# Attention and mixer in one kernel: the first unit gets a home of its own, and the five engine queues are drawn anew

## The chip, the cores and the metric

The kernel runs on one core of a Trainium2 chip. The metric is the device time of one execution in microseconds (us), as the median of several runs. TensorE is called PE here, VectorE DVE, ScalarE ACT, GpSimd POOL and SyncE SP, as in the profile. All arithmetic is fp32; the mixer's weights arrive as 64-bit floats and are turned into fp32 on the chip.

## The reference

There are two stages. The first is a delta-rule attention with 4 batches, 8 heads, 768 steps and head size 48: a state of 48 x 48 for each head, updated step by step. The second takes its output as tokens x of 4 x 768 x 384.

```python
k_n = k / (np.linalg.norm(k, axis=-1, keepdims=True) + 1e-06)
for t in range(S):
    y[:, :, t] = np.einsum('bhd,bhde->bhe', q[:, :, t], state)
    v_old = np.einsum('bhde,bhd->bhe', state, kt)
    state = state + bt[..., None] * np.einsum('bhd,bhe->bhde', kt, vt - v_old)
# x: y with the heads side by side, (4, 768, 384)
h = x.transpose(0, 2, 1) @ U @ V              # U (768, 32), V (32, 768)
u = x + h.transpose(0, 2, 1)
out = u + np.maximum(u @ w_ch1, 0.0) @ w_ch2  # 384 -> 1536 -> 384
```

## The kernel before

**Attention.** The work is cut into eight units: unit n is half of the sequence (`hf`) of batch `b`, n = 2b + hf, with six chunks of 64 steps for each of its heads. A unit loads k, q, v and z (k in the layout of the state update), takes norms (`norms`: a sqrt on ACT, L611, and the rest on DVE from L614), and forms two grams, k with k and q with k (`grams`): six matmuls by the identity turn a pair of chunks (L668), ACT copies the result into the unit's slot (L682), 24 calls of small matmuls form the products (L704), and DVE masks them (L717, L736). `blocks` inverts the unit lower triangular blocks: 30 pairs of DVE operations (L790, L796), transposes (L781, L803, L812), and joins on PE (L847 to L908) with ACT copies (L895, L914, L926). Then a recurrence over the chunks of each batch runs on PE (L972, L986, L1066, L1090, L1107, L1135) with DVE (L1120, L1147, L1149) and ACT (L956) between the steps. It writes the tokens into `X`.

**Weights.** The mixer's weights come in 14 slices (L1221: slice 0 is U and 1 is V, 2 to 7 are `w_ch1`, 8 to 13 `w_ch2`) into rotating rooms, by POOL's queue for slice 0 and by SP's for the others. DVE (L1244, L1250, L1256, L1262, L1272) and ACT (L1229) convert them; L1272 writes them into `w1_sb` and `w2_sb`. The loads of a slice are entries of part 78 up to `78.13`, its conversion an entry 14 higher (`78.21` is slice 7).

**Mixer.** There are twelve tiles of 256 tokens, three for each batch. A tile has a front (L1469 for the first tile of a batch, L1476 and L1486, the addition L1495 on DVE, and turning on PE at L1514 or, in quadrants, L405, with the ACT copy L1517 into `ut`), a wide product (L1580, or L393 in quadrants), a narrow product (L1695 or L393), and a sum L1620 with the store. The last five tiles take the first product in fewer steps (L1430), with sums of weights made on DVE. The matmuls run in several layouts of the PE array: full 128 rows, quadrants of 64, quarters of 32.

**Order.** Every engine works its instructions off in the order in which they stand in its queue. The program is written as about a hundred generators, the parts, each numbered. `ORDER` is a table with five queues, one for each engine, whose entries are numbers of parts: each entry lets that part issue its next operation on that engine. `11.2*2` is two operations of the third part that part 11 has started. A part waits in `need(...)` until keys such as `("rec", 0)` (batch 0's recurrence is done) or `("x", 0, c)` (a chunk's tokens are written) have been emitted. The order is thus fixed when the program is built; on the chip semaphores make the data dependences. The set `PARTED` lists the parts that use quadrants where both forms exist.

**Slots.** Two tiles of 9792 words for each partition hold a unit's data: `slots[n % 2]`. A unit's loads, in `load`, therefore wait for the unit two before:

```python
yield need(("rec", n - 2), ("used", n - 2), *[("x", b - 1, UC * hf + c) for c in range(UC)])
```

Units 0 and 2 share a slot, so unit 2's loads are issued at 80.5 to 90.3 us. The mixer's transposed tokens live in a rotating pair of tiles named `ut`.

Of the kernel before, what the change touches and what calls it, by code (L numbers as in the profile page):

```python
# [8 lines left out]
FP32 = mybir.dt.float32  # L9
# [9 lines left out]
DP = 64  # L19
# [7 lines left out]
def kernel(  # L27
# [68 lines left out]
    def dve(n):  # L96
        return (n + 151) / 960.0
# [16 lines left out]
    def need(*keys):  # L114
        return [key for key in keys if key[1] >= 0]
# [12 lines left out]
    def advance(i, value, at):  # L128
# [20 lines left out]
        9.0 9.1 9.0.0.0 9.1.0.0 2*2 19.0 19.1 3 19.0.0.0 3 19.1.0.0 10.0 10.1 10.0.0.0 20.0 11.4 10.1.0.0  # L149
        11.4 11.2*2 11.4*2 11.2*2 20.1 11.4*4 20.0.0.0 11.2*4 20.1.0.0 4.1 4.0*2 4.1 21.2*2 4 4.4 21.2 4  # L150
        21.2 4.5 4 21.4*2 21.2 4 4.5 4.6 4*2 21.2 4.6 21.2*2 4.7 4*2 4.8 4.7 4 21.4 4.9 4 21.4 4 4.9 4.8
        4.2*2 21.4*2 4 4.10 21.4*2 4*2 4.10 4.11 4*2 4.11 4.3 32.0 31.0 4.3 31.1 4.12 4 31.0.0.0 31.1.0.0 4
        4.12 32.1 4.13 4*2 4.13 4.14 4 4.15 4 4.14 4.15 79 32.0.0.0 81 32.1.0.0 81*2 40.0 82 98.0*2 39.0
        39.1 82 98.1 40.1 39.1.0.0 39.0.0.0 98.1 98.2 33.2*2 98.2 98.3*2 98.4 33.4*2 33.2 98.4 33.2 98.5
        33.4*2 33.2*2 98.5 98.7 83 33.2 33.4 33.2 33.4 98.7 33.4*2 98.8 5 5.0 5 40.1.0.0 5 98.8 5.1 5 98.9 5
        98.9 5 5.1 98.9 5 98.9 5.2 5 98.10 5 5.2 5.3 5 99.0 5 99.0 5 5.3 5.4 5 99.0 5 99.0 5.5 5 99.1*2 5
        5.4 99.1*2 5.5 40.0.0.0 5 83 99.2*2 99.3*2 99.4 48.0 99.4 41.2*2 47.0 99.7 47.1 47.0.0.0 47.1.0.0
        41.4*2 99.5*2 48.1 41.2 41.4*2 41.2 99.7 99.8 48.1.0.0 5 99.8 5.6 5 48.0.0.0 5 99.9 5 99.9 5.7 5*2
        99.9 5 5.6 99.9 5.8 5.7 5 99.10 5*2 100.0 5.9 5 100.0 5.8 5 100.0 5 100.0 5.9 5 5.10 5 100.1 5.11 5
        5.10 100.1 5 5.11 100.1*2 84 100.2*2 100.3*2 100.4*2 100.5 100.7 100.5 49.2*2 55.0.0.0 84 55.1.0.0  # L160
        100.7 100.8 49.2 49.4*2 49.2 100.8 84 100.9*2 6 85 100.9 6 100.9 56.0.0.0 56.1.0.0 6 100.10 49.4*2
        6.0 6 101.0*2 85 6.1 6 101.1*2 6 101.1 6 101.1 6.2 6 101.2*2 6.1 6 101.2*2 6 6.3 6.2 101.3 6 101.3 6
        6.4 6.3 6 101.4 6 101.4 6.5 6 101.4 6 101.4 6.4 6 6.5 101.5*2 101.7*2 57.2*2 57.4*2 86 57.4*2 57.2*2
        101.8*2 101.9*2 63.0.0.0 101.10 6 101.10 6 63.1.0.0 102.0*2 86 6.6 6 102.1*2 64.0.0.0 6 6.6 102.2 6
        102.2 6.7 6 102.2*2 6 6.7 102.3 6 102.3 6.8 6 102.3 6 102.3 6.9 6 102.4 6 102.4 6.8 6 102.4 6 102.4
        6.10 6 102.5*2 6.9 6.11 102.5 6 102.5 6.10 6 102.7 6.11 102.7 87 102.7*2 64.1.0.0 87 102.8*2 102.9*2
        102.10 71.0.0.0 103.0*2 71.1.0.0 103.1*2 103.2*2 103.3*2 65.4*2 65.2*2 103.4*2 72.1.0.0 65.2*2
        65.4*2 103.5*2 87 103.7 7 72.0.0.0 7 103.7 7 7.0 103.8*2 7.1 7 103.8*2 7 88 7 103.9*2 7 7.1 7.2 7
        103.10 7 7.2 104.0 7 104.0 7.3 7 104.0*2 7 7.3 7.4 104.1 7 104.1 7 104.1*2 7.5 7 7.4 104.2 7 104.2
        88 104.3*2 7 7.5 73.4*2 73.2*2 104.4*2 104.5 73.4*2 73.2*2 104.5 7 104.7 7 7.6 7 104.7 7 7.7 104.8  # L170
        7.6 7 104.8 7 104.8 7 104.8 7 7.7 7.8 7 104.9 7 7.8 7.9 7 104.9 7 89 7 104.10 7 7.9 7.10 7 7.11 7
        104.10 7 7.10 7.11 79 93.2 93.1 79 89 93.4 93.2 93.1 93.3 93.2 93.3 93.4 93.1 93.5 93.1 93.2 93.1
# [12 lines left out]
        78.20*2 21.4 78.21 21.4 78.21*4 4 78.22*2 4 78.22*2 4 78.22 4 78.23*2 4 78.23*3 78.24*5 4 78.25*2
        31.0.0.0*2 31.1.0.0*2 4 33 4 30 4 78.25 4 33*2 4 78.25*2 33*2 78.26 32.0.0.0 78.26 81 33 78.26 81
        32.1.0.0*2 78.26 33 78.26 33 82 33*2 32.0.0.0 30 33*8 33.4 33.2 78.26.1*3 39.0.0.0 78.27 98.2.1*3
        39.1.0.0 78.26.1 39.0.0.0 30 78.27*4 39.1.0.0 33.2*3 33.4*2 78.27.1 33.4 41 98.5.1*2 78.27.1*2
        98.7.0 98.5.1 78.27.1 38 83 41 98.6 5 98.7.1 41*3 38 98.8.0 5 98.8.1 41*3 5 41 5 41*2 40.1.0.0
        98.9.0 41 98.9.1 5 40.1.0.0 41 98.10.0 5 41*2 5 41 5 41*2 5 41 5 41*15 41.2 5 99.2.1 40.0.0.0 99.2.1  # L190
        38 40.0.0.0 99.2.1 99.7.0 41.4 47.0.0.0*2 47.1.0.0*2 49 99.5.1*3 46 49*2 46 49*2 99.7.1 99.8.0 99.6
        5 48.1.0.0*2 99.8.1 49*2 48.0.0.0 5 48.0.0.0 49 5 49*2 5 49*2 5 99.9.0 49*2 99.9.1 49 99.10.0 5 49 5
        49*2 5 49 5 49*2 5 49 5 49*9 46 49*2 84 49 100.2.1*2 49.2 49.4 55.1.0 55.0.0 100.5.1*2 100.2.1
        100.5.1 100.7.0 84 55.1.0.0 55.0.0.0 55.1.0.0 100.7.1 55.0.0.0 100.6 57 100.8.0 54 100.8.1 56.0.0
        57*4 56.1.0 6 85 100.9.0 56.0.0.0 56.1.0.0 56.0.0.0 6 57 56.1.0.0 100.9.1 100.10.0 57*7 6 57 6 57*2
        6 57*2 6 57*3 101.2.1 57 6 57 6 57*2 6 57 6 57*5 6 54 57*3 57.2 101.2.1 101.7.0 57.4 101.2.1
        101.5.1*3 101.7.1 54 86 101.6 101.8.0 101.8.1 63.0.0 64.0.0 101.9.0 101.9.1 63.1.0 63.0.0.0 6
        63.0.0.0 101.10.1 101.10.0 64.1.0 63.1.0.0*2 65 62 65*2 6 65 64.0.0.0 62 6 64.0.0.0 65*2 6 65*2 6
        65*3 6 65 6 102.2.1 65 6 65 6 65*3 6 102.2.1*2 65 6 65 102.5.1*2 65 62 87 65 102.5.1 102.7.0 65*3
        102.7.1 65 102.8.0 65 102.6 102.8.1 87 65 102.9.0 65 71.0.0 65 102.9.1 102.10.0 64.1.0.0*2 71.1.0  # L200
        65*4 71.1.0.0 65 71.0.0.0 65.4 71.0.0.0 71.1.0.0 65.2 73 72.1.0 72.0.0 70 73*2 72.1.0.0 103.2.1 73
        72.1.0.0 73*3 103.2.1*2 73 103.7.0 103.5.1*2 72.0.0.0 73 7 103.5.1 103.7.1 73 72.0.0.0 7 73 103.6
        73*2 7 103.8.0 88 103.8.1 73 7 73*2 103.9.0 73*2 7 73 103.10.0 103.9.1 7 73*2 7 73*2 7 73*2 70 7
        73*3 7 73*6 73.2 73.4 7 70 80*3 104.2.1*2 80 104.2.1 104.5.1 7 80*2 93.0*2 104.5.1 7 104.7.0 104.5.1
        104.7.1 7 104.6 7*2 93.0 104.8.0 104.8.1 7 93.0 104.9.0 7 80 7 104.9.1 7 89 93.0 7*2 93.0*2 80
        93.0*2 80*2 93.0 80 104.10.0 80 93.2.1 94.0*3 80 93.1.1 93.0 80 93.3.1 93.2.2 93.1.2 93.1.3 104.10.1
        93.2.3 93.5.0 94.0 93.1.4 94.0*6 93.4.1 90 94.2.1 90 105.0*3 94.3.1 94.1.1 105.1 94.1.2 94.2.2
        105.1*2 105.3.1 105.3.0 95.0 94.1.3 95.0*4 94.5.0 94.2.3 95.0 105.4.0 94.0 105.2 94.4.1 95.0 105.4.1
# [1568 lines left out]
```

## Time and profile before

| | |
|---|---|
| time, median of 3 runs | 590.49 us (590.03 to 590.49) |
| profiled execution | 589.15 us, span 587.4 us |
| mean granted PE clock | 0.939 |
| busy: PE, DVE, ACT, POOL | 545.3, 456.2, 227.3, 118.1 us |
| first DVE operation of batch 0's recurrence (L1149) | 59.47 us |
| its last (L1120) | 110.89 us |
| first front, L1469 | 113.50 us |
| first wide product, L1580 | 121.49 us |

Times within the profile are counted from the first instruction of the span. A line such as `L790` is the line of the kernel that issued the instruction. In a list of waits, the engine that stood idle is to the left of the arrow and what released it to the right, followed by the sum, the number and the longest.

### The profile page before, as it was taken

What the parts mean: (1) busy time and instruction counts of PE and PEld (TensorE: products, weight loads), DVE (VectorE), ACT (ScalarE), POOL (GpSimd) and SP (SyncE); (2) the same over time, 40 slices, a digit from 0 to 9 for tenths busy, and PEclk for the clock granted to TensorE, in tenths of its full rate; (3) what the DMA queues carried; (4) which work ended last, traced back from release to release, by engine and by line L of the source; (5) the groups of instructions that cost most, each with busy time, mean ns of one, the idle gap of its engine ahead of it and who ended that gap; (6) DMA issues with size and microseconds to landing.
All of it is one profiled execution on the core that took longest, in us unless ns stands there. A gap on an engine that the chain in (4) does not pass through costs nothing.

```text
span 587.4 us, 25542 instructions
## 1 busy us (share of the span) xinstructions
PE 545.3 (93%) x11460; PEld 491.1 (84%) x11460; DVE 456.2 (78%) x1086; ACT 227.3 (39%) x483; POOL 118.1 (20%) x205
## 2 busy tenths in 40 slices
PE   5697778799999999999999999999999999999997
PEld 4586677588888987997897798988889999999997
DVE  6898999999899898899878888888547574555552
ACT  4447476544433623344344305324423422131220
POOL 8132050311205304340252253301000000000000
PEclk9576666799999999999999999999999999999999
DMA  9634676652104314223212433200000000000013
GB/s 157 85 76 128 192 188 166 134 91 63 29 4 83 68 22 83 74 53 63 48 30 61 80 75 71 60 29 3 2 5 1 2 1 1 1 2 1 1 42 119
DMA packets 79213, 35.17 MB, mean 60 GB/s; under 512 B 65600, under 2 KB 76992, under 8 KB 79104
## 3 DMA queue, kind: packets, MB, share of 16 engines
q1 hardware_dynamic: 71200, 24.10, 18.9%
q0 software_dynamic: 6304, 9.15, 7.2%
q8 instruction: 90, 1.47, 1.0%
q10 hardware_dynamic: 1600, 0.30, 0.3%
q14 instruction: 19, 0.16, 0.1%
HBM read 28.80 MB, written 4.72 MB: 57 GB/s over the span
## 4 chain that ended last, share of the span: by engine, by line
PE 79%; DVE 7%; ACT 5%; DMA 4%; issue 3%; SPq 1%; POOL 1%; DVEq 0%; ACTq 0%; POOLq 0%
PE P L1695 24%; PE P L1580 12%; PE P L1430 12%; PE P L393 10%; PE P L704 3%; DMA wide<-in_moe_w_ch_dram 2%; PE P L668 2%; PE P L1066 2%; PE P L1090 1%; PE P L972 1%; PE P L1486 1%; PE P L986 1%; PE P L1135 1%; PE P L1514 1%; PE P L861 1%
## 5 line engine op out<-in xcount | busy, mean ns | idle before, releaser
L1695 PE MATMUL P<-w_sb,hs 128*128 128x192 f32 x480 | 84.2, 329 | 0.1
L1580 PE MATMUL P<-ut,w_sb 128*128 128x256 f32 x348 | 81.8, 386 | 0.1
L1695 PEld LDWEIGHTS P<-w_sb,hs 128*128 128x128 f32 x480 | 77.7, 190 | 1.3 <-issue 0.3
L1580 PEld LDWEIGHTS P<-ut,w_sb 128*128 128x128 f32 x348 | 64.1, 190 | 9.4 <-issue 0.6
L796 DVE TENSOR_TENSOR xt<-xt,prod 128x112 f32<-128x112 f32 (+21 forms) x200 | 64.6, 323 | 6.9
L790 DVE TENSOR_TENSOR prod<-gs,xt 128x112 f32<-128x112 f32 (+21 forms) x200 | 63.7, 319 | 3.9
L1620 DVE TENSOR_TENSOR X<-X,P 128x192 f32<-128x192 f32 x86 | 29.6, 349 | 36.1 <-PE P L1695 34.2
L1545 ACT ACTIVATE hs<-P 128x512 f32<-128x512 f32 x42 | 24.8, 597 | 62.1 <-PE P L1580 51.0
L393 PE MATMUL P<-ut,w_sb 64*64 64x256 f32 x624 | 43.0, 384 | 1.2 <-ACT hs L1545 0.9
L956 ACT COPY X<-P 64x192 f32<-64x192 f32 x96 | 30.0, 312 | 28.8 <-PE P L986 27.2
L704 PE MATMUL P<-slot 48*64 48x64 f32 x1536 | 33.5, 245 | 1.9 <-ACT slot L682 1.6
L704 PEld LDWEIGHTS P<-slot 48*64 48x64 f32 x1536 | 30.0, 157 | 6.1 <-ACT slot L682 2.5
L933 POOL MEMSET slot<- 32x384 f32 x32 | 13.4, 420 | 102.6 <-PE P L890 40.4
L1412 DVE TENSOR_TENSOR hs<-hs,P 128x512 f32<-128x512 f32 x30 | 20.1, 684 | 17.5 <-PE P L1430 9.2
L1695 PE MATMUL P<-w_sb,S 128*128 128x192 f32 x192 | 33.7, 330 | 0.0
L926 ACT COPY slot<-zz 32x384 f32<-32x384 f32 x64 | 32.3, 508 | 1.0
L1099 ACT COPY z<-P 128x192 f32<-128x192 f32 x36 | 11.5, 319 | 53.3 <-PE P L1090 46.4
L1695 PEld LDWEIGHTS P<-w_sb,S 128*128 128x128 f32 x192 | 31.1, 190 | 0.6 <-DVE xt L796 0.3
L548 POOL DMA_DIRECT2D slot<-in_k_dram x44 | 28.7, 657 | 12.3 <-PE P L1135 10.6
L668 PE MATMUL P<-ident,slot 128*128 128x128 f32 x108 | 20.0, 343 | 11.3 <-DMA slot<-in_k_dram 5.7
L1430 PE MATMUL P<-slot 128*128 128x128 f32 x240 | 29.7, 276 | 0.0
L1695 PE MATMUL P<-w_sb,slot 128*128 128x192 f32 x168 | 29.1, 327 | 0.0
(171 smaller groups left out, 1140.9 us busy)
## 6 DMA issues: line engine op xcount, KB each, us to landing
out_dram<-X SPq DMA_DIRECT2D x22, 192.0 KB, 2.0
X<-in_moe_w_ch_dram SPq DMA_DIRECT2D x10, 384.0 KB, 4.4
wide<-in_moe_w_ch_dram SPq DMA_DIRECT2D x10, 384.0 KB, 4.4
slot<-in_k_dram SPq DMA_DIRECT2D x48, 72.0 KB, 3.7
slot<-in_k_dram POOLq DMA_DIRECT2D x44, 72.0 KB, 3.1
slot<-in_v_dram SPq DMA_DIRECT2D x32, 72.0 KB, 3.7
slot<-in_v_dram POOLq DMA_DIRECT2D x32, 72.0 KB, 3.2
hs<-in_moe_w_ch_dram SPq DMA_DIRECT2D x4, 384.0 KB, 5.7
```

What stands on the lines that cost most here:

```text
L393: nc.tensor.matmul(to[half(g)], w[half(r), half(g)], x[half(r)], start=start, stop=stop, skip_group_check=True,)
L548: queue.dma_start(out=t[half(1 - g if name == "z" else g), :, to, 0:D], in_=src[b, 4 * g + s, hf * UC * L : (hf + 1) * UC * L, :].rearrang ...
L668: nc.tensor.transpose(p_t[:, c // 3, c % 3], t[:, c, 2 * j : 2 * j + 2].rearrange("p s d -> p (s d)"), ident,)
L704: nc.tensor.matmul(p_g[half(g ^ (par * i)), par, c], kq[rows, c, j, 0, half(g)], kq[rows, c, j, i, half(g)], start=True, stop=True,)
L790: nc.vector.tensor_tensor(out=prod, in0=gb[:, :, j : j + 1, j + 1 :].to_broadcast([128, split, m, w]), in1=xb[:, :, 0:m, j : j + 1].to_bro ...
L796: nc.vector.tensor_tensor(out=xb[:, :, 0:m, j + 1 :], in0=xb[:, :, 0:m, j + 1 :], in1=prod, op=ALU.subtract,)
L926: nc.scalar.copy(pg[quarter(i), :, at, :, a : a + BK], cut(zc, h)[quarter(i)].rearrange("p r (c j) t -> p r c j t", j=2),)
L956: nc.scalar.copy(x[half(c % 2), c // 2, 4 * D * g : 4 * D * (g + 1)].rearrange("p (j r d) -> p r j d", r=2, d=D), states(p_y)[half(g)],)
L1430: nc.tensor.matmul(bank[:, q], w_block(w)[:, q // 2, 128 * (q % 2) : 128 * (q % 2) + 128], token(b, i, t), start=c == 0 and q == 0, stop=True,
L1580: nc.tensor.matmul(p_f[:, x], w(x, t), ut[:, t], start=(t == 0), stop=(t == KT - 1))
L1620: nc.vector.tensor_tensor(out=to, in0=to, in1=p, op=ALU.add)
L1695: nc.tensor.matmul(to, of[0], of[1], start=of[2], stop=of[3], skip_group_check=True)
```

## The change

The first unit no longer lives in slot 0. Its large arrays go into `w2_sb`, its q and v into a new constant tile `uts_sb`, and its z into the last slice of `w1_sb`. The rotating `ut` of the mixer becomes the two halves of `uts_sb`. Unit 2 has slot 0 to itself: its loads wait only for two memsets, which a new part `pads` issues on POOL (they clear the padding columns, which unit 0's memsets cleared before). The last step of the weight slices from number 7 on, which writes where unit 0 lives, waits for unit 0's end. All five queues and `PARTED` are drawn anew; part numbers from 80 on are one higher.

```diff
+    w1_sb = const.tile([128, FT // 2, KT * 256], FP32, name="w1_sb")
+    w2_sb = const.tile([128, PRODUCTS, HF, HD], FP32, name="w2_sb")
+    uts_sb = const.tile([128, 2, KT, GT], FP32, name="uts_sb")
+
-    def views(slot):
+    def views(slot, q_room=None, z_room=None):
+        q_room = slot[:, 7680:9216] if q_room is None else q_room
+        z_room = slot[:, 9216 : 9216 + 2 * UC * D] if z_room is None else z_room
...
     units = [views(slots[n % 2]) for n in range(N)]
+    units[0] = views(
+        w2_sb.rearrange("p a f d -> p (a f d)"), uts_sb.rearrange("p y t n -> p (y t n)"),
+        w1_sb[:, FT // 2 - 1, 0 : 2 * UC * D],
+    )
...
+    def pads():
+        yield op("pool", 0.6)
+        nc.gpsimd.memset(units[2][0][:, :, :, D:DP], 0.0)
+        yield op("pool", 0.6)
+        nc.gpsimd.memset(units[2][4][:, :, :, D:DP], 0.0)
+        emitted("pads", 0.1)
...
-        yield need(("rec", n - 2), ("used", n - 2), *[("x", b - 1, UC * hf + c) for c in range(UC)])
+        if n != NU:
+            yield need(("rec", n - 2), ("used", n - 2), *[("x", b - 1, UC * hf + c) for c in range(UC)])
+        else:
+            yield ["pads"]
...
             emitted(("freed", i))
+            if i >= 7:
+                yield need(("rec", 0), ("used", 0), *[("x", 0, c) for c in range(UC)])
             yield op("dve", dve(n), port=True)
...
-        ut = uts[b, i] = mix.tile([128, KT, GT], FP32, name="ut")
+        ut = uts[b, i] = uts_sb[:, (NG * b + i) % 2]
...
+        begin(pads(), 5)
```

In the queues, part 1 is unit 0's k with the warm-up sqrt, 2 is beta, 8 unit 0's norms, 9 and 10 its grams, 11 its blocks, 18 to 21 the same for unit 1, 30 to 33 for unit 2. Parts 12 to 17 load unit 0's q, v and z, 22 to 29 unit 1's k, q, v and z, and 34 to 37 unit 2's. The first lines of three queues, before and after:

```diff
         act="""
-        1*4 9.0.0 1 9.1.0 9.0.0.0 9.1.0.0 78.14.0 2*2 9.0.0.0*2 8 19.0.0 9.0.0.0 9.1.0.0*3 19.0.0.0 19.1.0
...
+        1*4 9.0.0 9.1.0 9.0.0.0 9.1.0.0*2 2*2 9.1.0.0 8 9.0.0.0*3 9.1.0.0 1 19.0.0 3 19.1.0 19.0.0.0 10.1.0
+        10.0.0 20.0.0 3 19.0.0.0 78.14.0 19.1.0.0*2 11.4.0 11.2 18 11.4 11.4.0 11.2.0*2 11.3*3 11.4 11.1
+        19.1.0.0 20.1.0 11.2 31.0.0 19.0.0.0 32.0.0 11.3 78.15.0 11.4 11.1*3 11.2*2 11.4 19.1.0.0 31.1.0
+        19.0.0.0 4.0 32.1.0 4.0 21.2.0 4.1*2 21.2 78.16.0 4.4*2 21.2.0 78.17.0 21.1 21.4 78.18.0 21.2 21.1
...
         pool="""
-        11.0 13 23 78.0 2*3 17 23 25 23 13 23 25 13*2 25 29 25 21.0 15*2 29 17 15*2 11.3 11.1 11.3 11.1 27*4
...
+        11.0 80 78.0 23 25 23 80 2*3 23 13 23 13 17 13 25 13 15 21.0 15 25 34 35*2 34 35 17 35 15 25 31.0 29
...
         sp="""
-        0*4 78.1 22*2 12*2 22*2 78.1*2 12 78.1 12 24*3 14*4 24 16 26*4 78.2*2 28 16 78.3*2 78.4*2 28 78.5*2
...
+        0*4 22 24 34 12 22*3 24 12*2 35 12 78.1 35 78.1 24 35 14 24 14 34 78.1 16 34 78.1 35 34 26 14*2 16
```

More of the change, by code (lines that the diff above doesn't have):

```diff
@@ new lines @@
+        33.4*2 33.2 99.5 99.7 33.2 99.7 33.4 33.2*2 84 33.4 5 5.0 5 33.4*2 99.8 5 99.8 5.1 5 40.1.0.0 5 99.9
+        5 99.9 5.1 5 99.9*2 5.2 5*2 99.10 5 5.2 5.3 5 100.0*2 5 5.3 100.0 5 100.0 5.4 5 100.1 5.5 5 5.4
+        100.1 5 100.1 5.5 100.1 5 40.0.0.0 100.2*2 100.3*2 84 100.4 48.0 100.4 41.2*2 47.0 47.1 100.7
+        47.1.0.0 47.0.0.0 41.4*2 100.5*2 48.1 41.2 41.4 41.2 41.4 100.7 100.8 48.1.0.0 5 100.8 48.0.0.0 5
+        5.6 100.9 5 100.9 5 100.9 5 5.7 5 100.9 5 5.6 100.10 5.7 5 5.8 5 101.0 5 5.8 5.9 101.0 5*2 101.0*2 5
@@ new lines @@
+        78.20 21.4 78.21 21.4 78.21 21.4 78.21*3 4 78.22*2 4 78.22*2 4 78.22 4 78.23*5 4 78.24*5 4 78.25
+        31.0.0.0 4 31.0.0.0 78.25 31.1.0.0*2 4 33 4 78.25 4 78.25 4 78.25 30 33*4 82 33*2 82 33*4 32.0.0.0
+        32.1.0.0 78.26 32.1.0.0 32.0.0.0 78.26*2 33*2 78.26 83 33 78.26 78.26.1 33*4 30 39.1.0.0*2 78.26.1
+        33.2 78.27*3 99.2.1 78.27 99.2.1 78.27 33.4 39.0.0.0 33.2*2 39.0.0.0 33.2 78.27.1 78.26.1 41 30
+        78.27.1 78.26.1 33.4 99.7.0 33.4*2 99.5.1 78.27.1 99.5.1 78.27.1 84 99.5.1 99.2.1 5 99.7.1 38 41*2
@@ new lines @@
+        101.6 101.8.0 101.8.1 54 57 56.0.0 57 86 56.1.0 6 101.9.0 57*2 6 56.0.0.0 56.1.0.0*2 101.9.1
+        101.10.0 57*8 56.0.0.0 6 57 6 57*2 6 57 6 57*2 6 57*3 6 57*4 6 57 6 57*7 57.4 57.2 102.7.0 102.2.1
+        102.5.1 102.2.1*2 6 102.5.1*2 54 102.7.1 87 54 102.6 102.8.0 102.8.1 63.0.0 102.9.0 63.1.0 64.0.0
+        102.9.1 63.0.0.0 6 63.0.0.0 63.1.0.0*2 102.10.1 65 102.10.0 62 64.1.0 65 6 65*2 6 64.0.0.0*2 6 65 6
+        65*5 6 65 6 65*2 6 65 6 65*2 103.2.1 6 65*2 6 65 103.2.1 65 103.2.1 103.5.1*2 65 103.5.1 65 103.7.0
@@ new lines @@
+        4.6 21.4.0 4.5 21.1 4.6 4.5 21.4.0 78.19.0 21.2*2 4.7*2 21.1 78.20.0 4.8*2 78.21.0 4.9*2 4.2*2
+        21.3*4 21.4 78.22.0 21.4*2 4.10*2 78.23.0 4.11 4.3*2 78.24.0 4.11 31.0.0.0 31.1.0.0 4.12*2 78.25.0
+        31.0.0.0 31.1.0.0 4.13 30 4.13 4.14 4.15*2 4.14 82 99.0.0 78.26.0 39.0.0 99.1.0 39.1.0 40.1.0 40.0.0
+        39.1.0.0 99.2.0 39.1.0.0 39.0.0.0 33.2 78.27.0 83 99.3.0 39.0.0.0 99.4.0 33.1 33.4 33.1*2 99.5.0
+        33.2 33.1 33.2*2 38 33.3 5 33.4*2 5.0 33.4 33.3*2 5.0 5 99.9 33.3 5 5.1*2 5 5.2 100.0 5.2 5.3*2 5
@@ new lines @@
+        26 78.2*2 26*2 78.3 36 78.3 36 78.4*2 78.5*2 78.6 36 78.6 78.7 28 78.7 78.8*2 78.9 28 78.9 78.10*2
+        78.11*2 78.12 37*2 78.12 78.13 43*2 36 42 78.13 42*3 43*2 44*4 45*2 50 51*4 99.10.0 50*3 52 53 52*3
+        111*8 59*2 99.9.1 58 53 59*2 61 59*3 61 58*3 59 60 100.9.1 60*2 101.9.1 60 112*8 67*8 102.9.1 66*2
+        69 68*3 100.10.0 101.10.0 113*8 66 75 77 68 75 77 75 102.10.1 74*2 69 75 66 75 74 75 74 75*2
+        103.10.0 76*4 104.10.0 103.9.1 104.9.1 110.3.1 106.6.0 107.5.1 105.10.1 108.6.0 109.5.1 106.5.1
@@ L439, in views @@
         qk = slot[:, 6144:7680].rearrange("p (r c j t) -> p r c j t", r=2, c=UC, j=2)
-        qn = slot[:, 7680:9216].rearrange("p (c s d) -> p c s d", c=UC, s=4)
-        vn = slot[:, 7680 : 7680 + CS * D].rearrange("p (c s d) -> p c s d", c=UC, s=4)
-        kz = slot[:, 9216 : 9216 + 2 * UC * D].rearrange("p (c j d) -> p c j d", c=UC, j=2)
+        qn = q_room.rearrange("p (c s d) -> p c s d", c=UC, s=4)
+        vn = q_room[:, 0 : CS * D].rearrange("p (c s d) -> p c s d", c=UC, s=4)
+        kz = z_room.rearrange("p (c j d) -> p c j d", c=UC, j=2)
         diag = slot[:, 6144 : 6144 + BK * BK].rearrange("p (q t) -> p q t", t=BK)
@@ L474 @@
     nc.vector.memset(beta_rows, 0.0)
-    w1_sb = const.tile([128, FT // 2, KT * 256], FP32, name="w1_sb")
     u_sb = const.tile([128, NB, R], FP32, name="u_sb")
     v_sb = const.tile([128, S], FP32, name="v_sb")
-    w2_sb = const.tile([128, PRODUCTS, HF, HD], FP32, name="w2_sb")
     hs = const.tile([128, FT, GT], FP32, name="hs")
```

177 lines of the change are left out of this document (73 added, 104 removed), and 3 rows, old and new, of the table pe.

## The prediction

> **What bounds the kernel now.** I read the page's slices first, then busy time by stretch, then the waits of DVE, the chain of waits, and the timelines of the places that the diff moves. The slices, 14.7 us each:
>
> ```profile
> PE   5697778799999999999999999999999999999997
> DVE  6898999999899898899878888888547574555552
> PEclk9576666799999999999999999999999999999999
> DMA  9634676652104314223212433200000000000013
> ```
>
> PE is full from the ninth slice (about 118 us) to the end. Ahead of that DVE is, with PE at a low clock. The stretches say it in us (columns: length, busy time of PE, PEld, DVE, ACT, POOL, granted clock, DMA share, GB/s):
>
> ```profile
> 30.00:60.00 30.00, 24.37 (x885) 22.76 (x882) 27.42 (x68) 18.67 (x39) 7.86 (x14) 0.70 0.46 113
> 60.00:90.00 30.00, 21.99 (x776) 20.09 (x776) 29.06 (x50) 17.48 (x36) 8.59 (x14) 0.64 0.69 182
> 90.00:121.50 31.50, 25.55 (x785) 21.27 (x785) 29.27 (x59) 17.93 (x33) 7.58 (x12) 0.74 0.74 152
> 200.00:587.40 387.40, 378.92 (x6758) 345.17 (x6747) 277.04 (x672) 125.31 (x284) 62.03 (x106) 1.00 0.17 37
> 44.00:52.00 8.00, 4.36 (x200) 3.97 (x196) 6.61 (x22) 7.84 (x16) 3.71 (x7) 0.50 0.67 174
> ```
>
> So the time is the moment at which PE becomes full, plus PE's work from there on. That moment is the first mixer tile's front: DVE adds the mixed tokens (L1495), PE turns them (L405), and the products with the first weight follow at 121.49.
>
> ```profile
> 117.83 0.95 DVE L1495 TENSOR_TENSOR X<-X,P 128x768 f32<-128x768 f32 x1
> 118.83 0.93 PE L405 MATMUL P<-ident,X 64*64 64x64 f32 x48 [1.31 <-DVE X L1495]
> ```
>
> PE waited 1.31 us for DVE there: what DVE does ahead of L1495 sets the moment. From 30 to 121.5 us DVE's waits are few:
>
> ```profile
> DVE slot L736 <- ACT slot L914: 0.9, 1, 0.9
> DVE power L1244 <- DMA X<-in_moe_w_ch_dram: 0.6, 1, 0.6
> DVE power L1244 <- DMA wide<-in_moe_w_ch_dram: 0.6, 2, 0.4
> ```
>
> The last two are 1.26 us (0.40 at 93.66, 0.22 at 102.09, 0.64 at 114.67) for three weight slices. Their cause stands in the chain, where SP's queue holds unit loads at L548 (its semaphore waits included) and the weight comes behind them:
>
> ```profile
> 86.57 1.75 SPq L548
> 89.03 4.53 DMA wide<-in_moe_w_ch_dram
> 97.76 4.20 DMA wide<-in_moe_w_ch_dram
> 109.47 5.11 DMA X<-in_moe_w_ch_dram
> ```
>
> **The change, part by part.** The profiled execution took 589.15 us (span 587.4, 1.75 around it); the median of three runs is 590.49, 1.34 more. I work on the profiled execution and add the difference to the median. The matmuls (5814 calls) and DVE operations (1086) are the same set; only places change, and two POOL memsets are added.
>
> *Unit 2 loads early.* Its k and q leave POOL's and SP's queues at 80 to 90 us and go behind the first loads. The weights behind them in SP's queue are no longer held: the three DVE waits go, -1.26 us. What is late next on DVE is the arithmetic itself, which has 29.06 of 30 us.
>
> *Unit 2's turning moves from 95 to 104 us into 45 to 58 us.* Four groups of six matmuls at L668 and four ACT copies at L682 of 0.80 us (774 to 832 ns over 18), 3.2 us on ACT. In 44 to 52 ACT has 7.84 of 8 us, and DVE's 0.94 us wait for an ACT copy (L914, at 52.10) says that ACT is on the path there; from 40 to 44 it has 1.03 of 4 us, from 52 to 60 3.95 of 8. Bounds: 0 (the idle stretches take all) to 3.2. Two copies stand ahead of the one that DVE waits for (1.6 us), and some of the idle time ahead can take them: I take +0.8. On PE the groups take 0.9 us at full clock and 1.51 at half clock, ahead of the second step of batch 0's recurrence: 0 (PE is idle 45% of 44 to 52) to 1.4; I take +0.5, the nearer end, as the step's products wait their turn behind one such group.
>
> *The first unit's norm.* The warm-up sqrt is drawn later on ACT, so the second table load comes directly before the norm's sqrt (L611):
>
> ```profile
> 6.56 1.28 ACT L559 ACT_TABLE_LOAD   x1
> 7.85 0.20 ACT L559 ACTIVATE warm<-warm 128x1 f32<-128x1 f32 x1
> 15.01 0.26 ACT L611 ACTIVATE norm<-gs 128x32 f32<-128x32 f32 x1 [0.37 <-DVE gs L781]
> ```
>
> At 6.56 it lay beside DMA waits; at 15 DVE waits for the sqrt. Price: 1.28, less up to the 0.37 that ACT idles there and some 0.3 of DVE work drawn ahead, more for beta, issued some 2 us later: 0.65 to 1.6, I take 1.2. Unit 0's transpose at L803 (ends 28.84) then comes 0.8 later. But unit 1's k, whose last load sets PE free at 20.13, is drawn ahead of other loads, about 2.4 us sooner (four or five loads fewer ahead of it, 384 packets and 0.52 us of all 16 queues each), so unit 1's grams are not late. Left at 35 us: +0.3. The Trainium skill (ScalarE: Activation LUTs, What ACT_TABLE_LOAD costs) gives a table switch 1.283 us of load and 1.38 us of drain. The trace has the load's 1.28 exactly; the copy ahead ends at 6.54 and the operation behind begins at 7.85, so no drain is seen. By the page the term would be about 2.6, the total 1.4 higher.
>
> *DVE's queue.* Counted in durations of the rows of before, 2.1 us of work that stood ahead of L1495 stands behind it: parts of a late weight slice 1.27 (L1250 and others), one L736 of 0.54, the rest small. In exchange nothing else comes ahead. -2.1. It is work that DVE finds room for after 121 us (35.5 of 38.5, later 71%).
>
> *At the front:* +0.3 +0.8 +0.5 -1.26 -2.1 = -1.76 for L1495. Can PE follow? Its front group L1469 starts at 113.50 behind 48 products of unit 2 (L704, 112.02, about 1.5 us for that group), which are now behind it; it can start as much sooner, and L1495 stays the later of the two.
>
> *PE afterwards.* Those 24 matmul calls (48 instructions) have to be done in the full stretch: such an L704 group takes 0.93 us at full clock (303.36): +0.9. PE changes between full 128-row and quadrant matmuls 107 times from the front on, 100 after. A change costs about 0.1 us: the step from a full L1695 to a quadrant matmul is 0.255 us where two L1695 are 0.163 apart; back it is 0.148, where the quadrant matmuls' own pace explains about 0.04. -0.65, bounds -0.3 and -1.1. PE's holes over 0.08 us after 117.5 us are 7.8 us in 24; a redrawn queue has others, +-1.5.
>
> *New waits that cost nothing:* the last DVE operation of slices 7 on waits for unit 0's end. Unit 0's last copy is at about 82 us; slice 7's last step in the DVE queue is at 87. The cover is 5 us; if it is gone, DVE stands and all behind it. The two POOL memsets stand in a POOL that is 20% busy. The q and k of unit 1 and 2 share DMA at 2.5 to 22.5 us, where it is full; unit 1's last q is drawn so late on POOL that it lands about 40, as PE needs it (41). Two of four loads of the mixer's V weight go later, not needed before 113.
>
> **Sum:** -1.76 +0.9 -0.65 = -1.5: 587.6 on the profiled execution, 589.0 on the median. A difference under 0.2% (1.2 us) is what a measurement of this kernel can't tell from none.
>
> **The rivals.** (1) *Slower: the first 60 us lose more than the rest regains.* Table load, beta, four ACT copies where ACT is full and turning on a cold PE are all ahead of the recurrence, whose first DVE operation (L1149) is at 59.47. The gains are -1.26 -2.1 +0.9 -0.65 = -3.1, so it is slower once the three losses sum to more than 3.1, that is L1149 and the step behind it together 3.1 late. With the upper half of each (1.4, not absorbed, 2.4 and 1.0: 4.8) it is +1.7: 592.2. For it: ACT's 7.84 of 8 and DVE's 27.42 of 30. Against: ACT's idle 3 us at 40 to 44. By the page's drain alone, with the other terms as I took them, it is 590.4.
> (2) *Faster by more.* ACT's idle stretches take the copies, the turning fits between and keeps PE's clock up: losses 0 to 0.3, 587.4 or less. The clock is 0.50 in 40 to 52 and 0.81 in 52 to 60, and the six L668 go from 1.51 to 0.9 us with it. The Trainium skill (TensorE: Matmul & The Clock Gate, Part 1) has the clock rise after about 3.4 us of sustained activity; by it more work on PE at 45 to 58 raises the clock. The trace has half clock at 54% busy, so the added 6 us there could tip it.
> (3) *Nothing.* DVE's work up to 118 us is the same in kind, unit 2's products are drawn at nearly the same place as before, and DVE waits come back under another name (the second half of the last slice still stands behind loads of units 2 and 3 in SP's queue): 590.5.
>
> **Chances.** The forecast 0.33 (its own range 588 to 590), rival 1 0.30 (591.5 to 593), the drain 0.02, rival 2 0.15 (586.5 to 587.8), rival 3 0.20 (589.5 to 591.5). Faster by over 0.2% (under 589.3): rival 2 and most of the forecast, 0.44. Same: the rest of it and rival 3, 0.23. Slower: rival 1 and the tail of 3, 0.33. The range 586.7 to 593.0 leaves out the ends of rivals 1 and 2.
>
> **What would show it.** Right: a table load next to the norm's sqrt at about 15 us and L614 near 16.5; L668 groups of unit 2 at 45 to 58; L1149 first at 60 to 61; no DVE wait over 0.2 us for a weight between 90 and 116; L1495 at about 116; 24 matmul calls of L704 behind the front. Wrong: L1149 after 62; a DVE wait at a slice's last step for unit 0; PE holes after 118 us of more than 10 us.

## The result and the profile after

The changed kernel takes 592.61 us in the median of 20 runs (590.33 to 595.52), the kernel before 590.49 us (20 runs, 589.66 to 592.23). The ratio is 1.0031, with a 95% interval of 1.0017 to 1.0044: slower by about 1.8 us, where 1.5 us faster was forecast. In two more sets of runs, on two chips, it was 1.0024 (1.0003 to 1.0045) and 1.0002 (0.9982 to 1.0023). Weighted by their intervals the three give 1.0022, give or take 0.0010.

The profiled execution after has a span of 591.4 us against 587.4. Its slices:

```profile
PE   5797878799999998999998999999999999999997
DVE  6889999899898888889877888779765564555452
PEclk9957756599999999999999999999999999999999
DMA  9645753651005205232222361210000000000004
```

The picture is as before: DVE carries the first 120 us and PE the rest. By stretches (columns as before: length, PE, PEld, DVE, ACT, POOL, clock, DMA share, GB/s):

```profile
30.00:60.00 30.00, 26.30 (x758) 24.59 (x762) 27.57 (x70) 18.43 (x35) 16.62 (x27) 0.66 0.49 121
60.00:90.00 30.00, 24.59 (x788) 22.54 (x792) 27.54 (x49) 19.29 (x39) 0.82 (x2) 0.59 0.62 183
90.00:121.50 31.50, 25.14 (x803) 21.23 (x797) 29.20 (x64) 13.86 (x28) 10.28 (x17) 0.58 0.62 146
```

DVE is busy 27.54 of 30 us from 60 to 90, where it was 29.06. Its waits from 30 to 121.5 us:

```profile
DVE z L1138 <- PE P L1125: 2.1, 4, 0.9
DVE zz L883 <- PE P L879: 0.9, 2, 0.5
DVE X L1515 <- PE P L1506: 0.7, 1, 0.7
DVE power L1280 <- ACT power L1247: 0.6, 2, 0.3
```

The waits for weights (1.26 us) are gone, as forecast. Waits for PE in the recurrence (L1138 and L883, which were L1120 and L865) stand in their place. Their size varies from profile to profile: all DVE waits for PE from 30 us to the front's addition sum to 0.7 to 3.1 us in the four profiles with the order of before ahead of the front, and to 2.3 to 6.0 us in the twelve of the new one.

The second table load is where it was expected. The timeline of ACT:

```profile
14.39 0.30 ACT L605 COPY beta_rows<-P 128x48 f32<-128x48 f32 x2 [0.53 <-PE P L597]
14.57 0.63 ACT L747 ACTIVATE hs<-w_sb,even 128x384 f32<-128x384 f32 x1
15.22 1.28 ACT L629 ACT_TABLE_LOAD   x1
16.51 0.26 ACT L629 ACTIVATE norm<-gs 128x32 f32<-128x32 f32 x1
```

The first front's addition (L1515, before L1495) begins at 117.58, 0.25 us sooner than in the profile before. DVE's and PE's timelines there:

```profile
115.48 0.35 DVE L1496 COPY tt<-P 128x192 f32<-128x192 f32 x1
117.58 0.95 DVE L1515 TENSOR_TENSOR X<-X,P 128x768 f32<-128x768 f32 x1 [0.68 <-PE P L1506]
```

```profile
115.88 1.55 PE L1506 MATMUL P<-tt,v_sb 64*64 64x192 f32 x16 [1.70 <-DVE tt L1496]
```

From there on PE has more holes than before. Its waits from 121.5 us to the end, first after (line, whom it waited for, sum, times, longest):

```profile
PE P L1084 <- DVE s L1165: 1.9, 4, 0.9
PE P L393 <- ACT hs L1565: 1.6, 6, 0.3
PE P L1084 <- issue: 1.5, 2, 1.3
PE P L1153 <- ACT z L1117: 1.1, 4, 0.4
PE P L1004 <- ACT z L1117: 1.0, 3, 0.5
PE P L926 <- issue: 0.6, 1, 0.6
```

and then the three longest of before:

```profile
PE P L972 <- DVE s L1147: 1.4, 3, 1.0
PE P L986 <- ACT z L1099: 1.2, 3, 0.5
PE P L393 <- ACT hs L1545: 1.1, 4, 0.4
```

Counted as holes over 0.08 us after 121 us, PE stood 11.2 us in 35 holes after and 6.5 us in 23 before. (PE's wait of 1.31 us for L1495 at 118.83, before, lies ahead of that and is not in it.) The kernel before had no hole of the kind "issue" there in its profile; two other profiles with its order (`room_old_order` and `before_late_warm` below) have 0.6 us each.

### The profile page after: what moved, and what is told of

It is laid out like the page before. It is cut to its first block, busy times and chain, and to the rows that moved or that the text cites. A ratio compares the mean times of both kernels' runs of the same rounds, so it can differ in the third digit from the quotient of the medians.

```text
span 591.4 us, 25510 instructions
## 1 busy us (share of the span) xinstructions
PE 550.4 (93%) x11454; PEld 497.3 (84%) x11454; DVE 454.5 (77%) x1086; ACT 225.5 (38%) x484; POOL 118.8 (20%) x207
## 4 chain that ended last, share of the span: by engine, by line
PE 72%; DVE 6%; ACT 2%; issue 2%; DVEq 0%; ACTq 0%
PE P L1715 23%; PE P L1450 11%; PE P L1600 11%; PE P L393 10%; PE P L722 3%; DVE prod L808 2%; DVE xt L814 2%; PE P L1506 2%; PE P L1108 1%; PE P L1084 1%; PE P L990 1%; PE P L1153 1%; PE P L1534 1%; PE P L1004 1%; ACT hs L1565 1%
## 5 line engine op out<-in xcount | busy, mean ns | idle before, releaser
L1600 PE MATMUL P<-uts_sb,w_sb 128*128 128x256 f32 x336 | 77.9, 384 | 0.6 <-ACT hs L1565 0.3
L1600 PEld LDWEIGHTS P<-uts_sb,w_sb 128*128 128x128 f32 x336 | 62.1, 190 | 9.3 <-ACT hs L1565 0.7
L393 PE MATMUL P<-uts_sb,w_sb 64*64 64x256 f32 x672 | 45.9, 384 | 1.7 <-ACT hs L1565 1.6
L951 POOL MEMSET slot<- 32x384 f32 x28 | 12.0, 428 | 122.1 <-PE P L908 72.0
L533 POOL DMA_DIRECT2D slot<-in_k_dram x24 | 14.7, 617 | 86.6 <-ACT z L1117 86.5
L944 ACT COPY slot<-zz 32x384 f32<-32x384 f32 x56 | 28.3, 508 | 6.4 <-DVE zz L821 2.8
L722 PE MATMUL P<-slot 48*64 48x64 f32 x1344 | 27.8, 237 | 1.5 <-ACT slot L700 1.0
L722 PEld LDWEIGHTS P<-slot 48*64 48x64 f32 x1344 | 25.1, 150 | 4.6 <-ACT slot L700 1.5
L1450 PEld LDWEIGHTS P<-slot 128*128 128x128 f32 x240 | 28.3, 192 | 0.1
```

The costliest lines, as they stand in the source:

```text
L393: nc.tensor.matmul(to[half(g)], w[half(r), half(g)], x[half(r)], start=start, stop=stop, skip_group_check=True,)
L722: nc.tensor.matmul(p_g[half(g ^ (par * i)), par, c], kq[rows, c, j, 0, half(g)], kq[rows, c, j, i, half(g)], start=True, stop=True,)
L944: nc.scalar.copy(pg[quarter(i), :, at, :, a : a + BK], cut(zc, h)[quarter(i)].rearrange("p r (c j) t -> p r c j t", j=2),)
L1450: nc.tensor.matmul(bank[:, q], w_block(w)[:, q // 2, 128 * (q % 2) : 128 * (q % 2) + 128], token(b, i, t), start=c == 0 and q == 0, stop=True,
L1600: nc.tensor.matmul(p_f[:, x], w(x, t), ut[:, t], start=(t == 0), stop=(t == KT - 1))
```

## Experiments

The holes and waits that an expectation names are those of the profiles at hand when it was written (the 1.1 and 0.9 us near 321 us are `early_warm`'s). In the experiments' kernels most line numbers are one lower than in the changed kernel.

**The table load alone.** `early_warm` moves one entry of ACT's queue (and was run twice more unedited):

```diff
-        1*4 9.0.0 9.1.0 9.0.0.0 9.1.0.0*2 2*2 9.1.0.0 8 9.0.0.0*3 9.1.0.0 1 19.0.0 ...
+        1*4 9.0.0 1 9.1.0 9.0.0.0 9.1.0.0*2 2*2 9.1.0.0 8 9.0.0.0*3 9.1.0.0 19.0.0 ...
```

> The changed kernel with one entry of ACT's queue moved: the warm-up sqrt, and with it the second table load, goes back to where it stood before the change (behind the first copy, at about 6.5 us). Theory T (PE's full stretch after the first front has more holes, 11.4 us against 6.5 us, and the first 120 us came out even): the first unit's norm is 1.5 us earlier (about 15.3 us), batch 0's recurrence starts 0 to 1 us earlier, and the whole is 0 to 0.7 us faster than the changed kernel, 592 us. Rival H (the late first unit is what costs the time): 590.5 us or less, by the 1.5 us and what follows from it.

Ratio to the kernel before: 0.9979 (0.9955 to 1.0003). The norm's first DVE operation came at 15.83 us instead of 16.80. The time spoke for H, but not against T: the profile's holes were still 10.3 us.

**Room, head and tail.** Since every queue is a list, the order could be cut at the first front's turning: all entries issued up to there from one order, the rest from the other.

> The changed kernel's rooms (first unit in the second weights' room, tokens in a constant tile, the weights' wait for unit 0, two memsets) with the five queues of the kernel before, the memsets put second in POOL's queue. Theories T and H: the same as the kernel before within 0.7 us, 590.5 us, since unit 2's loads still stand late in the queues. Rival R (the rooms themselves cost: the memsets on POOL, the weights' wait, a tile's place): over 591.5 us.

> The changed kernel's queues up to the turning of the first front (about 120 us) and from there the remaining entries in the order of the kernel before, with its choice of quadrant parts. Theory T: about the kernel before or up to 1 us faster, 589.5 to 590.5 us, with PE's holes after the front near 6.5 us. Rival H: 592 us or more, holes as in the changed kernel or not, since what was lost is lost ahead of the front.

> The reverse: the queues of the kernel before up to the turning of the first front (the memsets put second in POOL's queue), and from there the remaining entries in the order of the changed kernel with its choice of quadrant parts. Theory T: slower than the kernel before by 1.5 to 3 us, 592 to 593.5 us, with PE's holes over 10 us. Rival H: 590.5 us or a little less (fewer changes of layout).

Ratios: room with the old order 1.0013 (0.9987 to 1.0038), new head with old tail 0.9996 (0.9972 to 1.0021), old head with new tail 1.0053 (1.0030 to 1.0075). The rooms show no cost that is clear of the noise, though up to 0.38% (2.2 us) could hide in the interval. On the old head the new order behind the front costs 0.40%, give or take 0.34, beside the rooms alone. That is theory T. On the new head the old order behind the front gains 0.26%, taking 1.0022 for the changed kernel, with an interval as wide. The old tail behind the new head has a stall of its own, at the first wide product. PE's waits with new head and old tail:

```profile
PE P L1505 <- DVE tt L1495: 1.7, 1, 1.7
PE P L1599 <- issue: 1.6, 1, 1.6
```

**The stores.** In the new tail ACT's copy of batch 2's first tokens into `X` waits for a store out of the same room, and PE stalls within one group of matmuls at the same moment:

```profile
ACT X L974 <- DMA out_dram<-X: 1.4, 1, 1.4
```

```profile
321.02 0.32 PE L1084 MATMUL P<-s,slot 48*64 48x48 f32 x7
322.61 0.37 PE L1084 MATMUL P<-s,slot 48*64 48x48 f32 x9 [1.27 <-issue]
```

> The changed kernel once more, unedited, as the partner of the others on this chip. 1.003 of the kernel before, as measured. A second profile shows whether the PE stall at 321 us inside one group of matmuls (L1084), which the profile calls issue, and ACT's wait for a store of tokens beside it come again: theory T says they do, at the same instructions; if they were chance, they don't.

Ratio 1.0024 (1.0003 to 1.0045). Both waits came again at the same instructions (1.5 and 1.4 us).

```diff
         sp="""
-        ... 67*8 102.9.1 66*2 69 68*3 100.10.0 101.10.0 113*8 ...
+        ... 67*8 100.10.0 101.10.0 102.9.1 66*2 69 68*3 113*8 ...
```

> The changed kernel with the warm-up sqrt early (as in early_warm), and in SP's queue the two stores of batch 0's second and third tile moved ahead of the store of batch 1's first tile and of unit 6's loads of k, z and v, behind which they stood until 315 us. Theory T (the new queue puts these stores so late that ACT's write of batch 2's tokens into the same room waits for them and PE's instruction fetch meets the full DMA queues): ACT's wait of 1.1 us for the store and PE's stall of 0.9 us in L1084 are gone, 1 to 1.8 us faster than early_warm. Rival (the stall is only hidden slack, or comes from the number of instructions alone): same time as early_warm within 0.5 us, the stall still there.

Ratio 1.0002 (0.9982 to 1.0022), beside 0.9979, 0.9994 and 0.9997 for `early_warm`: no gain. ACT's wait for the store was gone, and PE's stall was still there:

```profile
PE P L1083 <- issue: 0.6, 1, 0.6
PE P L989 <- ACT X L973: 0.6, 1, 0.6
```

So the stores were not the cause of the stall, and taking ACT's wait away bought no time. The theory fell in this part.

**Early warm-up and old tail together.**

> The changed kernel's queues up to the first front with the warm-up sqrt early, then the order of the kernel before. If early warm-up (about 1.5 to 3 us) and old order behind the front (about 2 us) add: 0.995 of the kernel before, about 3 us faster, and 4.5 us faster than the changed kernel. Rival (the early moment of the front is lost again in the full stretch, because DVE's postponed work comes due there): 0.999 to 1.000.

Ratio 0.9971 (0.9955 to 0.9986), median 590.99 us beside 592.28 for the kernel before on that chip. This version beats both kernels: the one before by some 1.7 us, and the changed one, which took 594.09 us in the same set (`after_again`), by 3.1 us.

> As warm_old_tail, and the norm's sqrt is put ahead of the two copies of beta and one copy of the gram in ACT's queue. In early_warm ACT idled 1.99 us for beta's matmuls and the sqrt came 0.5 us later than in the kernel before. Theory T: the norm 0.3 to 0.5 us earlier, up to 0.5 us faster than warm_old_tail. Rival: the norm waits for beta anyway, no change.

```diff
-        ... 9.1.0.0*2 2*2 9.1.0.0 8 9.0.0.0*3 ...
+        ... 9.1.0.0*2 8 2*2 9.1.0.0 9.0.0.0*3 ...
```

Ratio 0.9978 (0.9961 to 0.9994). The norm came 0.12 us earlier than in its partner's profile (15.48 against 15.60): no difference, nearer the rival.

**The load late in the old order.**

```diff
-        1*4 9.0.0 1 9.1.0 9.0.0.0 9.1.0.0 78.14.0 2*2 9.0.0.0*2 8 19.0.0 ...
+        1*4 9.0.0 9.1.0 9.0.0.0 9.1.0.0 78.14.0 2*2 9.0.0.0*2 8 1 19.0.0 ...
```

> The kernel before, unchanged but for one entry of ACT's queue: the warm-up sqrt, and with it the second table load, goes behind the norm's sqrt of unit 0, as the change has it. It prices that step alone. Theory T (what is lost at 15 us goes through to the first front, since DVE is full from 30 us on): unit 0's norm 1.2 to 1.5 us later, the first front's addition 1.2 to 2 us later, 1.002 to 1.0035 of the kernel before. Rival (the prediction's step: the wait for unit 1's k takes most of it up): 0.3 us or less, 1.0005.

Ratio 1.0000 (0.9978 to 1.0022). The norm was 1.82 us later, the recurrence's first DVE operation at 59.43 (59.47 in the profile before). In the old order the load is taken up ahead of the recurrence: the rival's case, as far as the interval reaches (up to 1.3 us could hide in it). The front's addition stood 2.16 us later than in the profile before, about as T had it, but 119.99 lies near the 119.35 and 119.85 of the two other profiles with the old order and an early load. What took the lateness up can be read row by row, since both kernels have the same DVE queue. The kernel before waits for ACT in three places, and these waits are gone here:

```profile
24.56 0.74 DVE L717 SCALAR_TENSOR_TENSOR slot<-P,even,slot 128x192 f32<-128x192 f32 x2 [0.23 <-ACT slot L714]
33.62 0.18 DVE L614 TENSOR_SCALAR norm<-norm 128x32 f32<-128x32 f32 x1 [0.46 <-ACT norm L611]
52.10 0.56 DVE L736 TENSOR_TENSOR slot<-P,mask_u 128x384 f32<-128x384 f32 x1 [0.94 <-ACT slot L914]
```

DVE is 1.82 us late ahead of the first, 1.50 behind it, 1.01 behind the second and no longer late behind the third.

**Filling holes.** Three swaps in PE's queue:

```diff
-        ... 5 99.9*2 5.2 5*2 99.10 ...    102.1*2 6*2 6.1 ...     6.7 6.8 103.3 6 103.3 ...
+        ... 5 99.9 5.2 5 99.9 5 99.10 ... 102.1 6 102.1 6 6.1 ... 6.7 103.3 6.8 6 103.3 ...
```

> early_warm with three swaps in PE's queue of the full stretch: a wide or narrow piece of 8 to 24 quadrant matmuls, which stood just before or after, goes between two steps of the recurrence that stood back to back at about 166, 269 and 321 us. Theory T (the new queue's holes are steps of the recurrence with too little other work between them): the holes of 0.55, 0.87 and 0.56 us shrink by about 1.5 us in sum, and the time from the front's addition to the end by as much: 0.997 to 0.998 of the kernel before if early_warm is at 1.000, about 1.5 us faster than early_warm. Rival (the recurrence itself is late and the holes come back at the next step): sum of holes and time as in early_warm.

> early_warm once more, unedited, as the partner of the filled version on this chip: 0.998 to 1.000 of the kernel before.

Ratios 0.9971 (0.9950 to 0.9991) and 0.9994 (0.9971 to 1.0017). The difference of 0.23% is the size that T expected, but the intervals overlap, and the 469.89 us from the front's addition to PE's last matmul lie within the 469.47 to 471.73 of `early_warm`: a gain is not shown. In the profiles the holes at 166 and 321 us went (0.55 and 0.56 us), the one at 269 stayed (0.86 us); in sum 9.9 us against 10.3, 11.6 and 9.8 in the three of `early_warm`. T holds for the holes on two of three places, and not for their sum.

**The load once and twice in the new order.** The last runs put the price on one chip and doubled it:

```diff
+    cold = const.tile([128, 1], FP32, name="cold")
...
         norm = small.tile([128, BK], FP32, name="norm")
+        if n == 0:
+            nc.scalar.activation(cold, warm, ACTF.Ln)
         nc.scalar.sqrt(norm, flat[:, 0 : BK * BK : BK + 1])
```

> The changed kernel, unedited, in one set of runs with early_warm_3 and late_twice, so that the price of the late table load in the new order comes from the same chip. 1.002 to 1.003 of the kernel before.

> The changed kernel with the warm-up sqrt early, unedited against early_warm. Theory P (in the new order nothing between 15 us and the first front takes the load's 1.5 us up): 1.5 us or more faster than after_3, 0.998 to 1.000 of the kernel before. Rival A (it is taken up, as the prediction had it and as the kernel before does): within 0.5 us of after_3.

> The changed kernel with one more function, a logarithm of a column of ones that nothing reads, put on ACT directly before the first unit's sqrt, so that two table loads stand there instead of one (the cost in question doubled). Theory P: the norm about 1.5 us later than in the changed kernel, batch 0's recurrence begins 1 to 1.5 us later, 1.005 to 1.006 of the kernel before. Rival A: the norm later by as much, the recurrence at the same time, 1.003. If the logarithm needs no load of its own, the norm is 0.2 us later and nothing else changes.

Ratios 1.0002 (0.9982 to 1.0023), 0.9997 (0.9981 to 1.0013) and 1.0047 (1.0027 to 1.0067). ACT's timeline with the load doubled:

```profile
15.70 1.28 ACT L631 ACT_TABLE_LOAD   x1
17.00 0.20 ACT L631 ACTIVATE cold<-warm 128x1 f32<-128x1 f32 x1
17.22 1.28 ACT L632 ACT_TABLE_LOAD   x1
18.51 0.26 ACT L632 ACTIVATE norm<-gs 128x32 f32<-128x32 f32 x1
```

The pair of after_3 and early_warm_3 by itself can't tell P from A (0.05%, give or take 0.26). Doubling can: the norm was 2.0 us later than in the changed kernel's first profile, the recurrence began at 63.31 us where the changed kernel's three profiles have 60.69 to 62.22, and the whole was 0.45% (give or take 0.29) slower than after_3. That is P: the second load costs 2.6 us, give or take 1.7, where it adds 1.5 at the norm. All three runs of each taken together, weighted by their intervals, `early_warm` stands at 0.9992 (give or take 0.0012) and the changed kernel at 1.0022 (0.0010): 1.8 us, give or take 0.9. The table below gives the moments in all profiles, in us; within a row they differ by the run-to-run spread of the first 120 us.

| order ahead of the front, warm-up | L1149 of before, first | L1495 of before, first |
|---|---|---|
| old | 59.47, 60.00, 59.55 | 117.83, 119.35, 119.85 |
| old, late load | 59.43 | 119.99 |
| new, late load (as changed) | 60.89, 62.22, 60.69, 60.17 | 117.58, 120.25, 118.04, 120.17 |
| new, early | 60.13, 60.90, 60.46, 59.37, 59.89, 58.95, 58.53 | 115.13, 118.15, 117.66, 114.86, 116.47, 116.62, 115.94 |
| new, load twice | 63.31 | 120.93 |

From the means, the recurrence begins 1.2 us later with the load late (61.0 against 59.7) and the front's addition is 2.6 us later (119.0 against 116.4). In the new order the load passes through. The DVE rows of `early_warm` and the changed kernel, whose DVE queue is the same too, say how: the norm is 0.97 us later in the changed kernel, and every DVE operation up to 35 us is late by as much (unit 1's norm is at 33.06 and 34.04), because DVE waits for nothing in between.

Profiles of one program differ by up to 3 us at the front, so the timed runs are the better measure of that moment. The time from the front's addition to PE's last matmul (3.05 us ahead of the span's end in every profile) differs less: it is 470.74, 470.21 and 470.24 us in the three profiles of the changed kernel, but 470.01, 471.73 and 469.47 in those of `early_warm`. The front's own shift is then the timed difference (ratio times 590.5 us) less the difference of that second part, against 467.6 us in the old order (mean of 466.56, 468.39 and 467.80):

| difference to the kernel before | timed, us | behind L1495 | front, timed less behind |
|---|---|---|---|
| changed kernel (three sets) | +1.3 | +2.8 | -1.5 |
| early warm-up (three sets) | -0.5 | +2.8 | -3.3 |
| new head, old tail | -0.2 | +2.3 | -2.5 |
| the same, early warm-up | -1.7 | +2.1 | -3.8 |
| old head, new tail | +3.1 | +2.2 | +0.9 |
| load twice | +2.8 | +3.4 | -0.6 |
| late load in the old order | 0.0 | +0.2 | -0.2 |

Each last number has an uncertainty of 1 to 1.5 us from the ratios' intervals, and more where one profile alone gives the middle column.

**Behind the front: busy or idle.** The same stretch can be split by the view of windows. Before and after (length, then PE's busy time, and further columns as in the stretches above):

```profile
117.83:584.39 466.56, 458.56 (x8810) 413.97 (x8810) 351.05 (x843) 160.68 (x356) 80.42 (x137) 1.00 0.18 40
117.58:588.32 470.74, 459.06 (x8896) 415.89 (x8888) 352.22 (x844) 159.69 (x358) 80.58 (x137) 1.00 0.18 38
```

With all profiles of each order (means, us; "issue" is idle time that nothing in the profile ends):

| ahead of the front, behind it | profiles | behind L1495 | PE busy | PE idle | of it issue |
|---|---|---|---|---|---|
| old, old | 3 | 467.6 | 458.7 | 8.9 | 0.4 |
| old, new | 1 | 469.8 | 456.8 | 13.1 | 1.0 |
| new, old (with and without early load) | 3 | 469.6 | 461.2 | 8.4 | 1.7 |
| new, new (the changed kernel) | 3 | 470.4 | 459.2 | 11.2 | 2.0 |

The new order behind the front saves PE 1.9 to 2.0 us of work and adds 2.8 to 4.2 us of idle time, on either head. The new order ahead of the front adds 2.5 us of work behind it and no idle time. Part of this work is the products of unit 2 (80 matmul instructions more of L704 in this stretch, some of them beside L1495, where PE stood idle before). Part is PE's clock, which in the new head is still low at the front. The first four us behind L1495, before and after:

```profile
117.83:121.83 4.00, 3.00 (x114) 2.50 (x115) 3.97 (x8) 1.60 (x2) 1.58 (x3) 1.00 1.29 169
117.58:121.58 4.00, 3.77 (x143) 3.53 (x136) 3.76 (x11) 0.80 (x1) 3.28 (x6) 0.73 1.21 213
```

The granted clock is 1.00 before and 0.73 after, and the turning at L405, 48 instructions in both, takes 0.93 us at 118.83 before and 1.44 us at 118.58 after.

## Why the prediction was wrong, point by point

**The bound.** Right: the moment of the first front and PE's work behind it make up the time. PE is busy 97 to 98% of the stretch behind L1495 in every profile.

**PE afterwards: the step that failed.** From the front's addition to PE's last matmul the changed kernel takes 2.8 us more than the old order, where +0.9 -0.65 = +0.25 was forecast, with +-1.5 for holes. PE's idle time there is 11.2 us in the mean of three profiles against 8.9: +2.3. So the term of holes, set at zero, is the one that was mis-sized, beyond its bounds, and the experiments put it on the new order behind the front, which adds idle time on both heads. Time that the profile calls issue is +1.6 of it; it comes with the new order on either side of the front (1.0 and 1.7 in the table). PE's wait for L1495 itself, 1.0 us of this stretch in the old order, is gone. So the other waits, most of them steps of the recurrence with too little between them, grew by about 1.6 too. "PE holes after 118 us of more than 10 us" stood among the signs that would make the prediction wrong, and the profile after has 11.2 us of them from 121 us on. PE's work itself came out at +0.5, near the forecast, but by luck: the new head added 2.5 us where +0.9 was counted, and the new order behind the front saved 1.9 to 2.0 where -0.65 was. Counted in the traces from L1495 on, the changes between 128-row matmuls and smaller ones go from 95 to 83, where the prediction had 107 and 100. PE's clock at the front was no term of the sum. The redrawn order behind the front was a term with bounds and not a rival; rival 1 had the outcome, and not this cause.

**The front: near in sum, by two errors.** The forecast for L1495 was -1.76; the timed runs give -1.5, with 1 to 1.5 us of uncertainty. The profiles alone don't show a shift (-0.25 in the first pair; in the table of moments the rows of the old order and of the changed one both have a mean of 119.0), so the nearness is not secured. Within it, two terms were off, one each way.

**The table load: a second step that failed.** The 1.2 us at the norm was 1.50. "Left at 35 us: +0.3" was wrong: the difference between early and late in the new order is 1.8 us (-3.3 against -1.5), so the 0.3 should have been the full 1.5. The prediction had unit 1's k as the cover. It did come sooner (its second group is turned at 16.27 instead of 20.13), but the new PE queue draws unit 0's q ahead of its product, which came 1.6 us later (26.90 against 25.27). PE's timeline after:

```profile
16.27 1.51 PE L686 MATMUL P<-ident,slot 128*128 128x128 f32 x6 [0.43 <-issue]
26.90 0.93 PE L722 MATMUL P<-slot 48*64 48x64 f32 x48
```

And before:

```profile
20.13 1.51 PE L668 MATMUL P<-ident,slot 128*128 128x128 f32 x6 [4.89 <-issue]
25.27 1.56 PE L704 MATMUL P<-slot 48*64 48x64 f32 x48 [0.64 <-ACT slot L682]
```

With the load early in the new order (`early_warm`) the product is at 26.18, so the load has 0.7 us of the lateness and the order the rest. What covers the load in the old order are DVE's three waits for ACT (0.23, 0.46 and 0.94 us, under `before_late_warm`). In the changed kernel's profile DVE has none of them.

**ACT and PE at 45 to 58 us.** Unit 2's four copies are at 46.21, 47.42, 53.66 and 58.49, and its turning from 45.30. With the load early the recurrence begins 0.1 us later than in the old order (59.75 against 59.67, the means of the table): the 0.8 didn't come, and the 0.5 behind it can't be seen in the front's -3.3. The clock did rise from 44 to 52 us, 0.93 instead of 0.50, as rival 2 had it; all twelve profiles of the new head have 0.65 to 1.00 there and all four of the old one 0.50. The Trainium skill (TensorE: Matmul & The Clock Gate, Part 1) has the clock rise with sustained activity, and the trace agrees. From 52 to 60 us the 0.60 of this profile is the lowest; the others of the new head have 0.67 to 0.83, as the old one (0.71 to 0.81). From 60 to 115 us the clock is lower, 0.58 instead of 0.67 (0.53 to 0.63 against 0.62 to 0.67 in all profiles), with unit 2's groups of six no longer there:

```profile
44.00:52.00 8.00, 5.75 (x242) 5.00 (x237) 7.31 (x21) 6.21 (x12) 3.41 (x7) 0.93 0.84 202
52.00:60.00 8.00, 6.65 (x206) 6.10 (x210) 7.79 (x15) 5.11 (x10) 0.98 (x1) 0.60 0.26 67
60.00:115.00 55.00, 44.34 (x1416) 38.92 (x1416) 51.33 (x95) 32.35 (x65) 5.40 (x10) 0.58 0.55 161
```

The cold PE is seen at the front: L1506 takes 1.55 us where the same 16 matmuls (L1486) took 0.82 at 116.70 before, and DVE's L1515 waits 0.68 us for it. That it also brought DVE's other waits for PE fits, but no run takes the clock alone.

**Unit 2's early loads.** Right in mechanism: with the load early the front is 3.3 us sooner, where -1.26 -2.1 +0.8 +0.5 = -2.1 was the sum without the table load. The waits for weights went (0.2 to 1.8 us in the four profiles of the old head, 0 to 0.3 in the new). DVE's busy time from 30 us to the front's addition is 79.6 us in the mean of seven profiles with the load early, against 81.9 in three of the old order: -2.3, where -2.1 was counted. What was not foreseen is that DVE's waits for PE grew (3.5 us in the mean of the same seven, 2.0 in the three), which is rival 3's mechanism in part.

**New waits that cost nothing.** Right: the last conversion step of slice 7 is at 88.20 after (87.64 before), and DVE has no wait there for unit 0. The rooms with the old order show no cost clear of the noise (1.0013, 0.9987 to 1.0038).

**The drain.** The Trainium skill (ScalarE: Activation LUTs, What ACT_TABLE_LOAD costs) has 1.38 us of drain with each switch. In every load here but the first of an execution, behind which ACT has to wait for PE's first product, the next operation begins 0.01 us behind the load's end and the load 0.01 to 0.02 us behind the operation ahead, two loads in a row with `late_twice` included. The measurement decides: 1.28 us.

## What to carry to other kernels

Where all queues are drawn anew, price the part behind the change as carefully as the part it is meant for: count where the chain's steps stand back to back, and forecast PE's busy and idle time there as two numbers, since one can hide the other's error. A stall that the old order takes up is covered only as long as that order's idle time is there: when the new order has no such wait, price the stall in full. And cut such a change in time as well as by feature; head and tail separate, and here the useful head (with one entry put back) and the old tail made a kernel faster than both.

## What the runs showed of the hardware

PE can stall within a group of like matmuls with nothing to wait for that the profile shows. At the same instructions of the new order behind the front (L1084 near 321 us) it stood 0.6 to 1.4 us in all ten profiles with that order, and with new head and old tail 1.3 to 2.0 us at the first wide product. The trace has PE's instructions arriving in pieces of 16 KB, 90 in an execution, one per 256 instructions on average. In all sixteen profiles PE has 51 holes of the kind issue of more than 0.3 us from 80 us on, and each of them ended 1.2 to 1.6 us after a piece had landed. Pieces come 6.6 us apart on average, so that chance would put about one hole in fifteen there. Late pieces are thus the likely cause, but no run changes the fetch alone, and why a piece comes late stays open.

The run-to-run spread (590.3 to 595.5 us for the changed kernel) lies in large part ahead of the first front, where its moment differs by 2.7 us between two profiles of the same program (117.58 and 120.25) and the time from there to PE's last matmul by 0.5 us (470.74 and 470.21). In `early_warm`'s three profiles both parts differ, by 3.0 us ahead and 2.3 us behind.
